# Unsplit f32 scores in every first-layer batch, fewer q/k buffers, more for probabilities, and two rows joined

## The chip, the cores and the metric

One Trainium2 chip, one core of it. The metric is the device time of one execution in microseconds (us); the median of three runs of the kernel before is 391.38 us (390.82 to 391.43).

## What is computed

Two layers of attention on 4 batches of 768 positions. The first has 8 heads of 64: each position sees the 128 positions up to itself and the first 4 ("sinks"). Its output, laid out as 768 x 512, is the input x of the second: 4 experts, each with its own q, k and v of 64, full causal attention, and a gate that keeps the best two experts per position.

```python
# first layer, per head
scores = scale * q @ k.T;  scores = where(is_sink | in_window, scores, -1e9)
a = softmax(scores);       x = a @ v
# second layer, per expert e
q, k, v = x @ wq[e], x @ wk[e], x @ wv[e]
a = softmax(where(causal, -1e9, scale * q @ k.T))
out += (gate weight of e, 0 unless in the top 2) * (a @ v @ wo[e])
```

## The kernel before

**Units.** The 768 positions are 6 row blocks of 128. Heads go in pairs: the two heads (or experts) of a pair sit on partitions 0 to 63 and 64 to 127, and their matmuls use the two halves of TensorE's rows. A first-layer *unit* is one pair of one batch (`first`, L1158; 16 of them), a second-layer unit one pair of experts of one batch (`second`, L1196; 8 of them). `ORD` and `LAST` (L1310) interleave them; in the last batch it is "0 p0 1 2 3 p1 c0 c1", where p is a second-layer unit of batch 2 and c one of batch 3, so the two last units of the program are c0 and c1.

**q and k.** For batches 0 and 1 (`EXACT`, L1306) the first layer uses q and k as they are, as f32: a `Pair` (L709) with `exact` keeps q in its load buffer `qn` and puts k, transposed, in `kx` (batch 0 transposes on TensorE, `turn_by_pe` L774; batch 1 on VectorE, L796). For batches 2 and 3 they are split into a rounded part (type float32r) and the rest: VectorE transposes in place (L800), ACT writes the rounded part (L801), POOL the rest (L805), into `qs` and `ks`. In `scores` (L810) an exact row is one f32 matmul per head (L817), which shows as two instructions in the trace; a split row is three matmuls per head (L822: high by high, high by low, low by high). The second layer always uses split q and k, which `put` (L746) makes from the projections (L1207).

**Rows of the first layer.** Row 0 sees one block, row 1 two (`edge_row`, L1070); rows 2 to 5 go two by two (`both_rows`, L1094). A score row covers 128 columns for row 0 and 260 for the others. Then VectorE adds the mask and takes the row's extreme, ACT takes the exponential, POOL multiplies by the reciprocal of the sum, TensorE transposes the probabilities (L875), ACT or VectorE copies them to `pt` (L704, L706), and TensorE multiplies by the values (L848) into an `acc` bank. One step does this for each row 0 and row 1 in `transposed` (L881).

**Rows of the second layer** (`wide_rows`, L970). Row i sees i+1 blocks. Rows of 5 and 6 blocks have their scores in two parts (`SPLIT`). Where a unit stands in `AWAY` (L1307; the first five second-layer units), rows 4 and 5 (of 5 and 6 blocks) are not transposed on TensorE: `by_way_of_dram` (L942) normalises on POOL into a second `p` buffer, transposes 32 x 32 pieces on VectorE (L958), stores to DRAM (`there`, L959) and loads four parts back (L955), and multiplies straight from `p`. In those units the row group 4 to 5 is done ahead of the group 0 to 3.

**What sets the order.** Nothing is issued in the order of the program text. `Plan` (L346) collects steps with an estimated cost per engine, dependencies, buffers to take and a priority; `emit` (L375) then simulates the engines and takes for each engine the step that can start first, for TensorE the one with the lowest priority after a price for waiting (`HURRY`) and for changing the mode of the array (`STAY`, `BULK`; "rows" for scores, "ROWS" for transposes, "cols" for the products with the values, "FULL"). Each step's priority is moved by a table of hand-set corrections, `NUDGE`. Where TensorE would wait, `emit` puts in multiplications by zero (`fill`, L513). A buffer kind is a ring of so many tiles (`kinds`, L507); a step that needs a new tile waits until all users of the old one are done. DMAs all go through SP's queue.

```python
def score_cost(n, exact=False):
    if exact:
        return 17 + 4 * n / 2.4
    return {128: 284, 256: 355, 260: 359, 384: 524, 512: 697}.get(n, 60 + 1.25 * n)
```

Of the kernel before, what the change touches and what calls it, by code (L numbers as in the profile page):

```python
# [10 lines left out]
F32 = mybir.dt.float32  # L11
F32R = mybir.dt.float32r
# [25 lines left out]
    "busy_PE": -35.2, " ": -14.5, " busy_PE": 44.4, " busy_PE 0": 14.4, "sink_values_DVE": -63.9, " sink_values_DVE": -42.7,  # L38
    "load_SP": -98.1, " load_SP": 27.8, "again_SP": -32.8, " again_SP": 2.5, "sink_values_ACT": -92.2,
    " sink_values_ACT": 34.2, "sink_values_POOL": -20.4, " sink_values_POOL": 18.3, "sink_values_SP": -68.0,  # L40
    " sink_values_SP": -27.3, "weight_ACT": 41.3, " weight_ACT": -64.4, "weight_POOL": -75.8, " weight_POOL": -39.4,
    "000 ": -57.8, "000 load_SP": 33.9, "tr_PE": -4.1, "000 tr_PE": -49.4, "000 tr_PE 0": -108.1, "fn_DVEACT": 23.4,
    "000 fn_DVEACT": 18.5, "000 tr_PE 1": -6.2, "go_POOL": -57.8, "000 go_POOL": 133.7, "000 tr_PE 2": 7.5,
    "000 tr_PE 3": 20.4, "spread_POOL": -50.7, "000 spread_POOL": -8.4, "differences_POOL": 173.3,
    "000 differences_POOL": -37.7, "band_scores_PE": 1.1, "000 band_scores_PE": -64.2, "000 band_scores_PE 0": -75.3,
    "low_DVE": -52.3, "000 low_DVE": 30.9, "exp_ACT": 274.5, "000 exp_ACT": 57.1, "go_DVE": -15.0, "000 go_DVE": 58.1,
    "norm_POOL": -83.7, "000 norm_POOL": 4.7, "000 tr_PE 4": -9.3, "av_PE": 1.6, "000 av_PE": -20.4, "000 av_PE 0": -24.7,
    "000 band_scores_PE 1": 14.2, "000 tr_PE 5": 30.2, "000 av_PE 1": -25.8, "000 band_scores_PE 2": 16.4,
    "pick_DVE": -15.0, "000 pick_DVE": 56.0, "000 band_scores_PE 3": 21.0, "keep_POOL": -105.0, "000 keep_POOL": 9.3,
    "000 tr_PE 6": -6.3, "tri_DVE": -17.0, "000 tri_DVE": -17.4, "of_sinks_PE": -0.7, "000 of_sinks_PE": -10.2,  # L50
# [26 lines left out]
    "110 load_SP": -51.3, "turn_DVE": 119.5, "110 turn_DVE": -77.7, "110 go_POOL": 93.6, "110 spread_POOL": 30.9,  # L77
# [210 lines left out]
}  # L288

HURRY = 29.29  # L290
STAY = 30.56
BULK = -8.87
FILL_COST, FILL_KEEP, FILL_END = 220.0, 0.0, 130000.0
# [177 lines left out]
def kernel(  # L471
# [15 lines left out]
    B, H, S, D = q.shape  # L487
    E = moe_wq.shape[0]
    Dm = H * D
    NB = S // 128  # L490
# [897 lines left out]
```

## Time and profile before

| | |
|---|---|
| median of the runs shown | 391.38 us |
| the profiled execution's own time | 391.6 us |
| its span, first to last instruction | 389.9 us |
| TensorE busy | 381.2 us (98%) |
| VectorE busy | 318.2 us (82%) |
| ACT busy | 263.4 us (68%) |
| POOL busy | 261.5 us (67%) |
| share of the chain that ended last on TensorE | 86% |
| DMA, share of 16 engines | 46.3% |

PE is TensorE's matmuls and PEld its weight loads; DVE is VectorE, ACT ScalarE, POOL GpSimd, SP the engine that issues DMAs. Busy time counts overlapping instructions of one engine once. Matmuls are pipelined: one starts while the one ahead still runs, and their ends are modelled. The chain that ended last follows the work back from the last instruction, at each step to what released it or to the instruction ahead of it on its engine.

### The profile page before, as it was taken

What the parts mean: (1) busy time and instruction counts of PE and PEld (TensorE: products, weight loads), DVE (VectorE), ACT (ScalarE), POOL (GpSimd) and SP (SyncE); (2) the same over time, 40 slices, a digit from 0 to 9 for tenths busy, and PEclk for the clock granted to TensorE, in tenths of its full rate; (3) what the DMA queues carried; (4) which work ended last, traced back from release to release, by engine and by line L of the source; (5) the groups of instructions that cost most, each with busy time, mean ns of one, the idle gap of its engine ahead of it and who ended that gap; (6) DMA issues with size and microseconds to landing.
All of it is one profiled execution on the core that took longest, in us unless ns stands there. A gap on an engine that the chain in (4) does not pass through costs nothing.

```text
span 389.9 us, 12672 instructions
## 1 busy us (share of the span) xinstructions
PE 381.2 (98%) x4276; PEld 318.4 (82%) x4276; DVE 318.2 (82%) x1422; ACT 263.4 (68%) x953; POOL 261.5 (67%) x461
## 2 busy tenths in 40 slices
PE   8999999999999999999998999999999999999996
PEld 7767788978788888878887789978888898987884
DVE  6898996799999889799689977789589826667953
ACT  4898876376988698188589848459778814507740
POOL 4879996378849968658949846499946730039940
PEclk9999999999999999999999999999999999999999
DMA  7979999045865855548915560269000000012003
GB/s 163 227 147 166 192 170 169 0 83 173 193 99 117 234 114 83 81 154 247 200 27 101 133 207 25 42 238 234 32 3 3 3 0 2 3 67 96 3 16 148
DMA packets 138432, 42.84 MB, mean 110 GB/s; under 512 B 122176, under 2 KB 132416, under 8 KB 138368
## 3 DMA queue, kind: packets, MB, share of 16 engines
q1 hardware_dynamic: 138368, 42.04, 46.3%
q8 instruction: 34, 0.56, 0.6%
q14 instruction: 30, 0.25, 0.2%
HBM read 28.25 MB, written 13.50 MB: 107 GB/s over the span
## 4 chain that ended last, share of the span: by engine, by line
PE 86%; ACT 7%; DVE 4%; issue 1%; POOL 0%; DVEq 0%; ACTq 0%
PE acc L848 20%; PE b L1207 18%; PE b L822 12%; PE b L875 9%; PE b L1234 9%; PE b L1281 9%; PE b L817 5%; ACT p L1014 2%; PE acc L852 2%; DVE p L1006 2%; ACT pt L704 1%; ACT p L1115 1%; PE b L1292 1%; PE b L521 1%; DVE p L1111 1%
## 5 line engine op out<-in xcount | busy, mean ns | idle before, releaser
L822 PE MATMUL b<-ks,qs 64*128 64x260 f32 (+4 forms) x672 | 72.6, 325 | 1.1 <-ACT pt L704 0.5
L1014 ACT ACTIVATE p<-p,st 128x128 f32<-128x128 f32 (+5 forms) x96 | 63.6, 668 | 13.6 <-DVE st L1006 13.1
L704 ACT ACTIVATE pt<-b 128x256 f32<-128x256 f32 (+3 forms) x156 | 55.1, 380 | 13.0 <-PE b L875 12.5
L1026 POOL TENSOR_TENSOR p<-p,st 128x128 f32<-128x128 f32 (+5 forms) x76 | 60.8, 823 | 1.3
L822 PEld LDWEIGHTS b<-ks,qs 64*128 64x128 f32 x672 | 52.9, 186 | 7.8 <-ACT pt L704 1.3
L1115 ACT ACTIVATE p<-p,st 128x132 f32<-128x132 f32 x128 | 50.8, 403 | 4.7 <-DVE st L1111 4.3
L875 PE MATMUL b<-ident,p 64*128 64x64 f32 x900 | 47.7, 228 | 0.0
L1006 DVE CUSTOM_DVE_ANT_0 p<-b,cmask 128x384 f32<-128x384 f32 (+3 forms) x96 | 45.3, 504 | 1.3 <-PE b L822 0.9
L875 PEld LDWEIGHTS b<-ident,p 64*128 64x128 f32 x900 | 37.6, 138 | 10.4 <-issue 4.8
L1089 POOL TENSOR_TENSOR p<-p,st 128x256 f32<-128x256 f32 (+1 forms) x32 | 26.4, 834 | 26.8 <-DVE st L864 7.9
L848 PE MATMUL acc<-pt,vn 128*64 128x128 f32 x448 | 42.8, 285 | 0.1
L1234 PE MATMUL b<-wvh,x 128*128 128x260 f32 x192 | 35.9, 285 | 0.0
L1207 PE MATMUL b<-x,wqh 128*128 128x512 f32 (+1 forms) x128 | 33.3, 345 | 0.0
L1111 DVE CUSTOM_DVE_ANT_0 p<-b,pair_mask 128x132 f32<-128x132 f32 x128 | 33.0, 286 | 0.3 <-POOL p L950 0.2
L1281 PE MATMUL b<-woh,y 128*128 128x512 f32 x96 | 32.8, 405 | 0.3 <-DVE st L1006 0.3
L1134 POOL TENSOR_TENSOR p<-p,st 128x512 f32<-128x512 f32 x32 | 33.0, 1041 | 0.0
L1207 PE MATMUL b<-x,wkh 128*128 128x512 f32 (+1 forms) x128 | 32.7, 342 | 0.0
L848 PE MATMUL acc<-pt,v 128*64 128x128 f32 x452 | 31.9, 279 | 0.1
L1082 ACT ACTIVATE p<-p,st 128x128 f32<-128x128 f32 (+1 forms) x64 | 28.7, 452 | 4.6 <-DVE st L1077 4.3
L1108 DVE COPY_PREDICATED b<-earlier,b 128x128 f32<-128x128 int32 x128 | 31.6, 286 | 0.1
L848 PEld LDWEIGHTS acc<-pt,vn 128*64 128x64 f32 x448 | 24.7, 136 | 7.8 <-issue 2.0
L1234 PEld LDWEIGHTS b<-wvh,x 128*128 128x128 f32 x192 | 30.0, 188 | 1.0 <-DVE st L1077 0.3
(136 smaller groups left out, 984.5 us busy)
## 6 DMA issues: line engine op xcount, KB each, us to landing
vn<-in_v_dram SPq DMA_DIRECT2D x32, 192.0 KB, 3.2
out_dram<-o SPq DMA_DIRECT2D x24, 256.0 KB, 2.2
qn<-in_q_dram SPq DMA_DIRECT2D x52, 96.0 KB, 2.4
kn<-in_k_dram SPq DMA_DIRECT2D x52, 96.0 KB, 2.7
there<-p SPq DMA_DIRECT2D x10, 384.0 KB, 3.2
p<-there SPq DMA_DIRECT2D x40, 96.0 KB, 2.4
there<-p SPq DMA_DIRECT2D x10, 320.0 KB, 2.3
p<-there SPq DMA_DIRECT2D x40, 80.0 KB, 2.8
```

What stands on the lines that cost most here:

```text
L704: nc.scalar.activation(dst(), src(), AF.Copy)
L822: nc.tensor.matmul(o, self.qs.t[hs, a, qs], self.ks.t[hs, b, ks], start=n == 0, stop=n == 2)
L848: nc.tensor.matmul(o[e * 64:e * 64 + 64], lhs, rhs, start=e not in self.begun, stop=last and self.done == len(self.steps))
L875: nc.tensor.transpose(t[g].t[:, n, :], x[gs], ident[gs, gs])
L1006: nc.vector.tensor_tensor_reduce(out=one(e)[:, cs], in0=s2[e].t[:, :(c1 - c0) * 128], in1=mask(c0, c1), scale=times, scalar=st.t[:, 3, es] ...
L1014: nc.scalar.activation(x, x, AF.Exp, bias=st.t[:, 0, es], scale=-1.0, accum_out=st.t[:, 1, es])
L1026: nc.gpsimd.tensor_mul(x, x, st.t[:, 2, e:e + 1].to_broadcast([128, n * 128]))
L1111: nc.vector.tensor_tensor_reduce(out=p.t[:, n, :], in0=s2[e].t[:, :SW], in1=pair_mask, scale=-scale, scalar=BIG, op0=OP.add, op1=OP.min, a ...
L1115: nc.scalar.activation(p.t[:, n, :], p.t[:, n, :], AF.Exp, bias=st.t[:, 0, n:n + 1], scale=-1.0, accum_out=st.t[:, 1, n:n + 1])
L1207: nc.tensor.matmul(t.t, w[a][:, c, es], X[b, c].t[:, x, cs], start=c == 0 and m == 0, stop=c == NCH - 1 and m == 2)
L1234: nc.tensor.matmul(t.t[:, :VW], X[b, c].t[:, a, qs], W["wv"][w][:, c, :], start=c == 0 and n == 0, stop=c == NCH - 1 and n == 2)
L1281: nc.tensor.matmul(t.t, Y[b, c].t[:, a, qs], W["wo"][w][:, c, :], start=c == 0 and n == 0, stop=c == EP - 1 and n == 2)
```

## The change

- `EXACT` takes in batches 2 and 3, so all first-layer scores are unsplit f32 matmuls; no first-layer unit uses `qs` or `ks` any more, and each of those two rings shrinks from 2 tiles to 1.
- The ring `p` of probabilities grows from 9 tiles to 13.
- In the five units of `AWAY`, row 3 (of 4 blocks) also goes through DRAM, beside rows 4 and 5.
- In `transposed`, the product step of row 0 is not issued by itself: it is kept in `acc.first` and issued with the step of row 1, in both layers.
- `HURRY`, `STAY` and `BULK` change, and so do nearly all entries of `NUDGE`; the kinds of entries for the splitting steps (`turn_ACT`, `low_POOL`) are gone, those for the joined step (`all_of_PE`) are new.

```diff
...
-HURRY = 29.29
-STAY = 30.56
-BULK = -8.87
+HURRY = 30.54
+STAY = 42.78
+BULK = -14.30
...
-    kinds = {"qn": (3, 768, F32), "kn": (2, 768, F32), "vn": (3, 768, F32), "qs": (2, 2 * S, F32R), "ks": (2, 2 * NB * SW, F32R),
-             "x": (6, 2 * S, F32R), "kx": (2, NB * SW, F32), "v2": (1, 1536, F32), "y0": (1, 2 * S, F32R), "y1": (1, 2 * S, F32R), "p": (9, 768, F32),
+    kinds = {"qn": (3, 768, F32), "kn": (2, 768, F32), "vn": (3, 768, F32), "qs": (1, 2 * S, F32R), "ks": (1, 2 * NB * SW, F32R),
+             "x": (6, 2 * S, F32R), "kx": (2, NB * SW, F32), "v2": (1, 1536, F32), "y0": (1, 2 * S, F32R), "y1": (1, 2 * S, F32R), "p": (13, 768, F32),
...
-            self.begun, self.steps, self.done = set(), [], 0
+            self.begun, self.steps, self.done, self.first = set(), [], 0, None
...
-        def av():
-            acc.done += 1
+        def av(n=n, cols=cols):
             for c, j in enumerate(cols):
                 for e in range(2):
                     acc.add(i, e, value[0](j, e), pt.t[:, 2 * c + e, :], 2 * c + 2 == n)
+        if i == 0 and TOGETHER:
+            acc.first = (av, moved, pt, n, cols)
+            return
+        made, before, pts, many, mine = [av], moved, [pt], n, cols
+        if acc.first:
+            made, before, pts, many, mine = [acc.first[0], av], acc.first[1] + moved, [acc.first[2], pt], n + acc.first[3], [*acc.first[4], *cols]
+            acc.first = None
+
+        def all_of():
+            acc.done += 1
+            for x in made:
+                x()
         new, used = acc.bufs()
-        acc.steps.append(plan.step(prio + AV_LAG, {PE: 109 * n}, av, moved + value[1](cols), new,
-                                   [pt] + value[2] + used, fifo="av", mode="cols"))
+        acc.steps.append(plan.step(prio + AV_LAG, {PE: 109 * many}, all_of, before + value[1](mine), new,
+                                   pts + value[2] + used, fifo="av", mode="cols"))
...
-    EXACT = (0, 1)
-    AWAY, MOVE = {u: (4, 5) for u in ((0, 0), (0, 1), (1, 0), (1, 1), (2, 0))}, 300
+    EXACT = (0, 1, 2, 3)
+    AWAY, MOVE = {u: (3, 4, 5) for u in ((0, 0), (0, 1), (1, 0), (1, 1), (2, 0))}, 300
+    TOGETHER = True
```

## Rows read from the trace of the kernel before

**Rows 1.** The page: the span; busy us, share of the span, instructions.
```profile
span 389.9 us, 12672 instructions
...
PE 381.2 (98%) x4276; PEld 318.4 (82%) x4276; DVE 318.2 (82%) x1422; ACT 263.4 (68%) x953; POOL 261.5 (67%) x461
```

**Rows 2.** Busy time by stretch, the last 22 us; the first line names the columns.
```profile
core 0: us, PE busy (x) PEld busy (x) DVE busy (x) ACT busy (x) POOL busy (x), PEclk, DMA share, GB/s
368.00:390.00 22.00, 18.16 (x206) 14.22 (x204) 11.32 (x27) 5.91 (x15) 6.08 (x7) 0.98 0.20 73
```

**Rows 3.** Timeline of TensorE: start, length, instruction; long score rows alone, L817 and L822.
```profile
64.65 0.71 PE L817 MATMUL b<-kx,qn 64*128 64x260 f32 x4
65.19 0.22 PE L875 MATMUL b<-ident,psk 64*128 64x64 f32 x2
...
138.08 0.63 PE L822 MATMUL b<-ks,qs 64*128 64x260 f32 x6
138.55 0.46 PE L875 MATMUL b<-ident,p 64*128 64x64 f32 x10
```

**Rows 4.** Groups of TensorE by form: count | busy us, mean ns | idle before.
```profile
L817 PE MATMUL b<-kx,qn 64*128 64x260 f32 x160 | 26.1, 408 | 0.1
...
L822 PE MATMUL b<-ks,qs 64*128 64x260 f32 x240 | 23.3, 305 | 0.2 <-DVE st L1077 0.2
```

**Rows 5.** Timeline of TensorE, short score rows alone.
```profile
63.61 0.49 PE L817 MATMUL b<-kx,qn 64*128 64x128 f32 x4
63.94 0.41 PE L875 MATMUL b<-ident,p 64*128 64x64 f32 x8
...
136.96 0.55 PE L822 MATMUL b<-ks,qs 64*128 64x128 f32 x6
137.35 0.37 PE L875 MATMUL b<-ident,p 64*128 64x64 f32 x6
```

**Rows 6.** Groups by form, POOL and ACT: the splitting of q.
```profile
L805 POOL TENSOR_TENSOR qs<-qn,qs 128x384 fp32r<-128x384 f32 x16 | 16.2, 1014 | 4.0 <-ACT qs L801 4.0
...
L801 ACT ACTIVATE qs<-qn 128x384 fp32r<-128x384 f32 x16 | 8.2, 516 | 0.0
```

**Rows 7.** Timeline of TensorE, 330 to 333 us: transposes and products in runs.
```profile
330.01 0.96 PE L875 MATMUL b<-ident,p 64*128 64x64 f32 x24
330.78 0.77 PE L822 MATMUL b<-ks,qs 64*128 64x384 f32 x6
331.49 1.53 PE L848 MATMUL acc<-pt,v 128*64 128x128 f32 x24
332.95 0.46 PE L875 MATMUL b<-ident,p 64*128 64x64 f32 x8
333.22 0.59 PE L822 MATMUL b<-ks,qs 64*128 64x384 f32 x4
```

**Rows 8.** Groups by form, VectorE: transposes on the way through DRAM.
```profile
L958 DVE STREAM_TRANSPOSE p<-p 128x640 f32<-128x640 f32 x10 | 8.3, 828 | 0.0
```

**Rows 9.** Busy time by stretch, 78 to 127 us, columns as in rows 2.
```profile
78.00:127.00 49.00, 48.79 (x589) 39.34 (x586) 48.22 (x216) 39.53 (x149) 37.77 (x67) 1.00 0.59 133
```

**Rows 10.** The DRAM tile: its issues on SP, ns min/median/max; time to landing.
```profile
L955 SPq DMA_DIRECT2D p<-there x80: 303/430/1963, 91.1 to 271.3; - x80
L959 SPq DMA_DIRECT2D there<-p x20: 319/344/1153, 88.0 to 262.7; - x20
...
DMA to landing us min/median/max: 2.0/2.6/5.2
```

**Rows 11.** Timeline of TensorE, 351.6 to 353.2 us: a lone step of row 0.
```profile
351.69 0.60 PE L822 MATMUL b<-ks,qs 64*128 64x256 f32 x6
352.36 0.44 PE L848 MATMUL acc<-pt,v 128*64 128x128 f32 x4
352.73 0.62 PE L822 MATMUL b<-ks,qs 64*128 64x256 f32 x6
353.19 0.28 PE L875 MATMUL b<-ident,p 64*128 64x64 f32 x4
```

**Rows 12.** Busy time by stretch of line L1207 alone; PE, PEld, clock, DMA.
```profile
308.00:325.00 17.00, 17.00 (x96) 14.60 (x96) 1.00 0.00 1
```

More of the change, by code (lines that the diff above doesn't have):

```diff
@@ L37 @@
 NUDGE = {
[L38 to L47, printed above, removed]
@@ L48 @@
-    "000 band_scores_PE 1": 14.2, "000 tr_PE 5": 30.2, "000 av_PE 1": -25.8, "000 band_scores_PE 2": 16.4,
-    "pick_DVE": -15.0, "000 pick_DVE": 56.0, "000 band_scores_PE 3": 21.0, "keep_POOL": -105.0, "000 keep_POOL": 9.3,
-    "000 tr_PE 6": -6.3, "tri_DVE": -17.0, "000 tri_DVE": -17.4, "of_sinks_PE": -0.7, "000 of_sinks_PE": -10.2,
[26 rows of a table removed]
-    "110 load_SP": -51.3, "turn_DVE": 119.5, "110 turn_DVE": -77.7, "110 go_POOL": 93.6, "110 spread_POOL": 30.9,
[20 rows of a table removed]
-    "most_DVE": -123.6, "001 most_DVE": -1.2, "rank_POOL": 48.2, "001 rank_POOL": 26.8, "values_ACT": -124.6,
@@ L99 @@
-    "001 values_ACT": -18.0, "weigh_DVE": -107.5, "001 weigh_DVE": -60.0, "proj_PE": -8.3, "001 proj_PE": -16.4,
[5 rows of a table removed]
-    "001 factor_POOL": 87.0, "001 norm_POOL": -120.4, "by_way_of_dram_DVE": -34.9, "001 by_way_of_dram_DVE": -73.8,
-    "by_way_of_dram_SP": -39.1, "001 by_way_of_dram_SP": 69.0, "back_SP": -58.9, "001 back_SP": -1.1, "001 av_PE": 13.4,
[30 rows of a table removed]
-    "turn_ACT": -12.9, "210 turn_ACT": 14.9, "low_POOL": 90.7, "210 low_POOL": 8.9, "210 go_POOL": -18.8,
[150 rows of a table removed]
-}
-HURRY = 29.29
-STAY = 30.56
-BULK = -8.87
+    "busy_PE": 33.5, " ": -40.9, " busy_PE": -16.2, " busy_PE 0": -17.8, "sink_values_DVE": -16.4,
@@ new lines @@
+    " sink_values_DVE": -55.9, "load_SP": 13.5, " load_SP": 92.9, "again_SP": 2.2, " again_SP": -33.1,
+    "sink_values_ACT": 70.0, " sink_values_ACT": -18.8, "sink_values_POOL": -19.7, " sink_values_POOL": -20.8,
+    "sink_values_SP": -9.5, " sink_values_SP": 1.4, "weight_ACT": 56.9, " weight_ACT": 25.6, "weight_POOL": 64.1,
+    " weight_POOL": -72.7, "000 ": -24.6, "000 load_SP": -68.6, "tr_PE": -1.3, "000 tr_PE": -25.9, "000 tr_PE 0": -51.6,
+    "fn_DVEACT": 41.8, "000 fn_DVEACT": -67.8, "000 tr_PE 1": -26.1, "go_POOL": -128.5, "000 go_POOL": -52.9,
@@ new lines @@
+    "000 tr_PE 2": 11.5, "000 tr_PE 3": 12.1, "spread_POOL": 72.3, "000 spread_POOL": 21.3, "differences_POOL": 139.4,
+    "000 differences_POOL": -18.7, "band_scores_PE": 1.9, "000 band_scores_PE": -43.2, "000 band_scores_PE 0": -2.3,
+    "low_DVE": 3.9, "000 low_DVE": -146.7, "exp_ACT": 300.6, "000 exp_ACT": -4.8, "go_DVE": 6.8, "000 go_DVE": -34.9,
[3 rows of a table added]
+    "tri_DVE": -18.1, "000 tri_DVE": 108.8, "of_sinks_PE": 0.4, "000 of_sinks_PE": -4.3, "000 of_sinks_PE 0": 6.5,
[47 rows of a table added]
+    "most_DVE": 89.8, "001 most_DVE": 48.2, "rank_POOL": 224.3, "001 rank_POOL": -59.8, "values_ACT": -79.4,
@@ L293 @@
+    "001 values_ACT": 24.7, "weigh_DVE": -61.0, "001 weigh_DVE": 68.2, "proj_PE": 7.3, "001 proj_PE": -6.9,
[5 rows of a table added]
+    "001 factor_POOL": 15.7, "001 norm_POOL": -46.2, "by_way_of_dram_DVE": -6.4, "001 by_way_of_dram_DVE": 3.5,
+    "by_way_of_dram_SP": -85.0, "001 by_way_of_dram_SP": 12.0, "back_SP": -83.2, "001 back_SP": -164.3, "001 av_PE": -3.8,
[175 rows of a table added]
+}
+HURRY = 30.54
+STAY = 42.78
+BULK = -14.30
 FILL_COST, FILL_KEEP, FILL_END = 220.0, 0.0, 130000.0
```

461 rows, old and new, of the table NUDGE are left out of this document.

## The prediction

> **What bounds the kernel now.** I read the page's busy times first: TensorE is busy 381.2 of 389.9 us [rows 1]. Then the table by stretch, where the last 22 us hold 18.2 of work and the granted clock stands at 0.98 to 1.00 of 2.4 GHz [rows 2, 9, 12]: 3.7 of the 8.7 idle us are the tail, and 5.0 us are left for the start and all waits between. The time is what TensorE has to do, plus a start and a tail, and an edit is worth what it takes from TensorE or adds to it. Time freed on ACT or POOL is worth something only inside those 5.0 us.
>
> TensorE time is read in the timeline as the distance from one start to the next: ends of matmuls overlap, starts don't.
>
> **Unsplit scores in batches 2 and 3.** Eight pairs of heads have one short row (128 columns) and five long ones (260) each. A long row alone, a transpose behind it, takes 65.19-64.65 = 0.54 us unsplit and 138.55-138.08 = 0.47 split: +0.07 [rows 3]. That is the one like-for-like pair, so I take it: 40 x 0.07 = +2.8. From above: unsplit matmuls last 408 ns in the mean, split ones 305 [rows 4]; if all of that 0.10 counted once per row, +4.1. From below: with four matmuls in place of six, nothing. A short row takes 63.94-63.61 = 0.33 unsplit, 137.35-136.96 = 0.39 split [rows 5]: 8 x -0.06 = -0.5. Together +2.3, bounds -0.5 and +4.1.
>
> The Trainium skill ("FP8 and Floating Point Precision", TensorE Precision Notes) says that a true FP32 matmul makes four passes through the array. Against the three products of the split this rule speaks against the edit: a third more than 0.47 is an estimate of +0.16 per long row, and with a third on short rows too some +7 us in place of +2.3. The lone rows of both lengths disagree with it in size; a mild form of it is a rival below.
>
> The splitting itself goes: 32 copies of 0.51 us on ACT and 32 subtractions of 1.01 us on POOL (those of qs stand in [rows 6], those of ks are as many and as long), 16 and 32 us. VectorE's transposes of q and k stay. TensorE waited little for any of it: bounds 0 and the 5.0 us of start and waits; I take -0.5, as most of the 5.0 must be the start, before anything is split. That q now stays in its load buffer until its scores are done delays later loads of q, which are issued a whole unit ahead: nothing, and a load's 2 to 5 us if that lead is gone.
>
> **Rows of 4 blocks through DRAM.** In five units such a row loses 16 transposes. 24 take 330.78-330.01 = 0.77, 8 take 333.22-332.95 = 0.27 [rows 7], so 16 take 0.50: 5 x 0.50 = -2.5. The bound beyond is -3.2, if a change of mode goes with each (0.13, below). The products behind them stay, in number and shape. New beside TensorE, per row: two VectorE transposes, two stores and eight loads on SP's queue; the two POOL multiplications write elsewhere but are as many. A transpose of 640 columns takes 0.83 [rows 8], so one of 512 some 0.66: +6.6 for ten on VectorE, against ten copies of 512 columns that go, from VectorE or ACT. VectorE has no room from 78 to 127, where two of these units lie (48.2 busy of 49 [rows 9]), and ACT has 9.5 us there: bounds 0 and +6.6, I take +0.5, because copies can move to ACT. SP issues a store in 0.34 and a load in 0.43 us [rows 10]: 2 x 0.34 + 8 x 0.43 = 4.1 per row. Behind them on that queue stand loads of q, k and v for the next units, issued a unit ahead, so nothing; without that lead 4.1 per unit. Row 3 is the last row of these units, and its part of y can't be finished until it is back from DRAM; the first-layer units that follow cover that.
>
> **Rows 0 and 1 in one step.** 17 of the 24 steps of row 0 (4 matmuls) stand alone between other modes, like the one at 352.36. It takes 352.73-352.36 = 0.37 [rows 11]. 24 in a run take 332.95-331.49 = 1.46 [rows 7], 0.061 each, so four more in a run cost 0.24: 0.13 is saved. The score ahead of it also pays: 352.36-351.69 = 0.67 into products, 353.19-352.73 = 0.46 into a transpose, so up to 0.21 more [rows 11]. 17 x 0.13 = 2.2 and 17 x 0.34 = 5.8 are the bounds; I take 0.20 each, -3.4, nearer the lower one, since not every lone step has a score ahead. The joined step waits for the copies of row 1 and holds two of three pt buffers until then; what is late next is a third transpose, and scores cover it.
>
> **One qs, one ks, 13 p.** Only the 8 second-layer units still use qs and ks. In batch 3 two of them follow each other; both are now projected in one stretch, 17 us from 308 on, 8.5 each [rows 12]. With one buffer the last projection must come behind the last score of the unit ahead, which now starts at 352.73 [rows 11]. A unit's scores take 2 x 1 + 4 x 2 = 10 buffers of p; nine were one too few, and 13 let these scores run on at 335. So the wait is covered by work that can change places (values and stores stand between). Bounds 0 and +8.5; I take 0.
>
> **The order** (new priorities, a change of mode priced at 42.8 for 30.6) is in no row. With some 90 stretches of products in the trace, one in ten more or fewer is 9 x 0.34 = 3.1 us either way. I take -0.5.
>
> Sum: +2.3 - 0.5 - 2.5 + 0.5 - 3.4 + 0 - 0.5 = -4.1. The profiled execution took 391.6, so 387.5; the median of the runs is 0.2 lower, so I forecast 387.3 us.
>
> **Rivals.** *Slower: the single buffers bind at the end.* Place: batch 3, from 325 on. If the scores of the unit ahead still end at 353, the last unit's projection starts there, its scores come 8.5 us later than now, and the tail behind them has nothing to run beside. It decides once other TensorE work that is ready there falls short. For it: the last 22 us already lack work [rows 2]. Against it: ten p are fewer than 13. 387.3 + 8.5 = 395.8, and slower once more than 4.9 of it is paid. Chance 0.14.
>
> *VectorE becomes the bound from 78 to 127* [rows 9]. There the transposes of two rows are paid (4 x 0.66 = 2.6) and their TensorE gain of 1.0 is lost; with the 0.5 already in the sum, +3.1: 390.4. With some four joined steps of that stretch (0.8) lost too, 391.2. Chance 0.10, taken as no change.
>
> *Dear scores.* Long rows at +0.10 and no gain in short ones: +4.1 for +2.3, 389.1. The Trainium skill's rule on FP32 passes, cited above, would give more, some 392 as an estimate. Chance 0.13, still faster.
>
> *More relief.* Freed POOL and ACT and four more p end all waits (-5.0 for -0.5) and the order is one in ten better: 387.3 - 4.5 - 2.6 = 380.2; half of it, 383.8. Chance 0.13. Against it: there is little waiting to end.
>
> That the change does not do what it says can be in one place: if the order put rows 0 and 1 together at little cost anyway, the 3.4 are not there, 390.7; that belongs to "no change".
>
> **How the numbers follow.** The forecast has 0.50. This kernel's measurement tells about 0.2% (0.8 us) from no change. Faster 0.50 + 0.13 + 0.13 = 0.76; within 0.10; slower 0.14. The range reaches from 383.0, inside the relief rival, to 392.3, past the VectorE rival into the slower one; left out are some 0.06 below and 0.12 above.
>
> **What would show it.** Right: no ACT or POOL line splits q or k; the unsplit group grows from 160 to 320 matmuls of 260 columns and the split one is gone; 80 fewer transposes of p; lone steps of four products nearly gone; TensorE's busy time about 4 us lower, with its idle time unchanged. Wrong: TensorE idle or on filler after 335 ahead of a projection; VectorE at its limit with TensorE waiting for it; a lone unsplit long row far from 0.54; as many changes of mode as now.

## The result and the profile after

The kernel after takes 387.44 us in the median of 4 runs (387.10 to 387.83), beside 391.33 for the kernel before. The ratio is 0.9902, with a 95% interval of 0.9888 to 0.9917: faster by 1.0%. The forecast was 387.3 us.

The page of the kernel after, the lines that answer to [rows 1]:

```profile
span 385.4 us, 12301 instructions
...
PE 375.7 (97%) x4124; PEld 315.0 (82%) x4124; DVE 317.5 (82%) x1416; ACT 252.7 (66%) x927; POOL 230.0 (60%) x429
```

TensorE is busy 5.5 us less; its idle time went from 8.7 to 9.7 us. VectorE has as much to do as before. ACT lost 10.7 us and POOL 31.5.

The groups by form that answer to [rows 4] and [rows 8], TensorE, then POOL and VectorE (count | busy us, mean ns | idle before):

```profile
L811 PE MATMUL b<-kx,qn 64*128 64x260 f32 x320 | 51.8, 410 | 0.6 <-POOL kx L763 0.3 <-ACT kx L698 0.3
L869 PE MATMUL b<-ident,p 64*128 64x64 f32 x820 | 43.0, 228 | 0.0
L842 PE MATMUL acc<-p,v 128*64 128x128 f32 x300 | 19.6, 276 | 0.9 <-DMA p<-there 0.9
...
L955 POOL TENSOR_TENSOR p<-p,st 128x512 f32<-128x512 f32 x10 | 10.2, 1040 | 0.7 <-PE b L869 0.6
...
L963 DVE STREAM_TRANSPOSE p<-p 128x512 f32<-128x512 f32 x10 | 7.0, 704 | 1.7 <-POOL p L955 1.4
```

All 320 long score matmuls are unsplit, and no split group of 260 columns is left. Two of TensorE's lone score rows, a long and a short one, with the transposes behind them, answer to [rows 3, 5]:

```profile
99.25 0.71 PE L811 MATMUL b<-kx,qn 64*128 64x260 f32 x4
99.79 0.28 PE L869 MATMUL b<-ident,p 64*128 64x64 f32 x4
...
191.31 0.44 PE L811 MATMUL b<-kx,qn 64*128 64x128 f32 x4
191.58 0.28 PE L869 MATMUL b<-ident,p 64*128 64x64 f32 x4
```

From start to start these are 0.54 and 0.27 us. The stretches that answer to [rows 9, 2], and between them the one in which the single qs and ks were to bind:

```profile
core 0: us, PE busy (x) PEld busy (x) DVE busy (x) ACT busy (x) POOL busy (x), PEclk, DMA share, GB/s
78.00:127.00 49.00, 47.97 (x590) 39.51 (x588) 47.12 (x206) 38.17 (x143) 35.84 (x64) 1.00 0.59 151
320.00:342.00 22.00, 22.00 (x176) 19.90 (x175) 12.30 (x49) 7.57 (x21) 1.29 (x5) 1.00 0.10 37
363.50:385.50 22.00, 18.15 (x223) 14.78 (x218) 9.01 (x20) 6.21 (x16) 5.71 (x6) 1.00 0.19 73
```

TensorE is full from 320 to 342, VectorE has 1.9 us of room in its densest stretch, and the tail is as it was. TensorE's waits after the change:

```profile
PE b L1297 <- DVE lanes L560: 1.1, 1, 1.1
PE acc L846 <- DVE x L686: 0.9, 1, 0.9
PE acc L842 <- DMA p<-there: 0.9, 1, 0.9
PE acc L842 <- DVE pt L700: 0.7, 1, 0.7
PE b L869 <- DMA kn<-in_k_dram: 0.5, 1, 0.5
```

No wait is for qs, ks or the splitting of q and k. This is where TensorE's time went: the distances from one matmul's start to the next, added up by kind over the whole trace (a wait counts with the matmul ahead of it):

| kind of matmul | before, us | after, us | difference |
| --- | --- | --- | --- |
| scores of 128 and 260 columns, split and not | 51.8 (x528) | 53.3 (x432) | +1.5 |
| other split scores | 37.9 | 37.1 | -0.8 |
| transposes | 45.5 (x1060) | 42.8 (x980) | -2.8 |
| products | 88.8 | 87.1 | -1.7 |
| sinks | 9.2 | 8.3 | -1.0 |
| projections, values, stores | 140.8 | 139.8 | -1.0 |
| fillers | 6.0 (x76) | 8.0 (x100) | +1.9 |
| matmuls on zeros at the start | 4.6 | 3.8 | -0.8 |

Before rounding they add up to -4.5 us. The first line holds 80 long rows, 42.5 us before and 43.3 after, and 24 short ones, 9.3 and 10.1. The last line is no work of the change: in another trace of the kernel after, with three psk buffers (below), the same 20 matmuls take 4.6 us again. Stretches of one mode went from 348 to 298, stretches of products from 89 to 71, and the 17 lone steps of four products are gone.

### The profile page after: what moved, and what is told of

Its sections match the earlier page's. It is cut to its first block, busy times and chain, and to the rows that moved or that the text cites. A ratio compares the mean times of both kernels' runs of the same rounds, so it can differ in the third digit from the quotient of the medians.

```text
span 385.4 us, 12301 instructions
## 1 busy us (share of the span) xinstructions
PE 375.7 (97%) x4124; PEld 315.0 (82%) x4124; DVE 317.5 (82%) x1416; ACT 252.7 (66%) x927; POOL 230.0 (60%) x429
## 4 chain that ended last, share of the span: by engine, by line
PE 76%; DVE 15%; ACT 3%; DMA 2%; issue 2%; SPq 1%; POOL 0%; DVEq 0%; ACTq 0%; POOLq 0%
PE b L1212 18%; PE acc L842 14%; PE b L1239 9%; PE b L1286 9%; PE b L811 9%; PE b L869 7%; PE b L816 6%; DVE p L1011 3%; DVE b L1113 2%; DVE p L1116 2%; DVE pt L924 1%; DVE x L686 1%; DVE p L963 1%; PE acc L846 1%; DMA kn<-in_k_dram 1%
## 5 line engine op out<-in xcount | busy, mean ns | idle before, releaser
L1019 ACT ACTIVATE p<-p,st 128x640 f32<-128x640 f32 (+5 forms) x96 | 63.7, 667 | 10.0 <-DVE st L1011 8.8
L811 PE MATMUL b<-kx,qn 64*128 64x260 f32 (+1 forms) x384 | 58.1, 393 | 0.8 <-ACT kx L698 0.4
L698 ACT ACTIVATE pt<-b 128x256 f32<-128x256 f32 (+2 forms) x158 | 53.3, 368 | 7.9 <-PE b L869 7.8
L1031 POOL TENSOR_TENSOR p<-p,st 128x128 f32<-128x128 f32 (+5 forms) x66 | 50.4, 787 | 0.6
L816 PE MATMUL b<-ks,qs 64*128 64x384 f32 (+3 forms) x384 | 45.2, 344 | 0.3 <-DVE st L1011 0.2
L869 PE MATMUL b<-ident,p 64*128 64x64 f32 x820 | 43.0, 228 | 0.0
L811 PEld LDWEIGHTS b<-kx,qn 64*128 64x128 f32 x384 | 34.8, 186 | 8.4 <-issue 1.2
L955 POOL TENSOR_TENSOR p<-p,st 128x640 f32<-128x640 f32 (+2 forms) x30 | 36.9, 1254 | 1.3 <-PE b L869 0.6
L816 PEld LDWEIGHTS b<-ks,qs 64*128 64x128 f32 x384 | 32.4, 186 | 4.8 <-issue 1.2
L1212 PE MATMUL b<-x,wkh 128*128 128x256 f32 (+1 forms) x128 | 33.4, 347 | 0.2 <-DVE st L1116 0.2
```

Source lines behind the costliest of these rows:

```text
L698: nc.scalar.activation(dst(), src(), AF.Copy)
L811: nc.tensor.matmul(o, self.q_of()[hs, qs], self.ks.t[hs, 0, ks], start=True, stop=True)
L816: nc.tensor.matmul(o, self.qs.t[hs, a, qs], self.ks.t[hs, b, ks], start=n == 0, stop=n == 2)
L869: nc.tensor.transpose(t[g].t[:, n, :], x[gs], ident[gs, gs])
L1019: nc.scalar.activation(x, x, AF.Exp, bias=st.t[:, 0, es], scale=-1.0, accum_out=st.t[:, 1, es])
L1031: nc.gpsimd.tensor_mul(x, x, st.t[:, 2, e:e + 1].to_broadcast([128, n * 128]))
```

## The experiments

In all but the first two, the order of the steps on each engine is the one recorded from the kernel named, and only the steps of the edit differ, placed where their inputs are ready or at a place given to them; so an edit meets the order of a kernel that was laid out without it. The first two keep the kernel's own planner, whose estimates don't count the second issue. "+x us" is against the kernel of that order: before as measured beside it, after as 0.9902 times that.

**What a score row costs.** The scores of the 40 long rows of batches 2 and 3 are issued twice, in each kernel:

```diff
-        lambda: pair.scores(...)
+        def scores_of():
+            for _ in range(2 if pair.twice and i else 1):
+                pair.scores(...)
```

> The kernel before, with the split scores of the 40 long first-layer rows of batches 2 and 3 issued twice in a row (same order otherwise, same output). Theory (TensorE's own work sets the time): each row adds its price in a run, six matmuls at some 0.35 us, so 40 x 0.35 = +14 us, about 405. Rival (TensorE has hidden room, other engines set the time): under half of that, below 398.

> The changed kernel, with the unsplit scores of the same 40 rows issued twice. Theory: the unsplit row is dearer than the split one by 0.07 to 0.10 us, so this adds 40 x 0.42 to 0.45 = 17 to 18 us, about 405, which is 2.8 to 4 more than the split rows add to the kernel before. If the four passes of f32 set the price, 4/3 of what the split rows add, 4.7 more. If the unsplit row is no dearer in a run, the same addition as in the kernel before.

Measured: 403.17 us split twice (ratio to before 1.0299, 1.0284 to 1.0313), +11.65 us or 0.29 a row; 400.80 us unsplit twice (1.0239, 1.0223 to 1.0256), +13.1 us or 0.33 a row. Both are less than was expected (14, and 17 to 18). In the two groups by form the count is right:

```profile
L822 PE MATMUL b<-ks,qs 64*128 64x260 f32 x480 | 36.1, 289 | 0.0
```

```profile
L811 PE MATMUL b<-kx,qn 64*128 64x260 f32 x480 | 67.7, 397 | 0.6 <-POOL kx L763 0.3 <-ACT kx L698 0.3
```

TensorE sets the time in both kernels: of the 12.5 and 15.8 us that its trace grew by from start to start, 11.65 and 13.1 came into the time. A row behind its like is dearer unsplit by 0.04 us of time (13.1/40 - 11.65/40), and by 0.08 from start to start (15.8/40 in the one trace, 12.5/40 in the other). For 40 rows that is 1.5 to 3.2 us, with the forecast's +2.8 for long rows inside. In the kernel after itself, where most rows don't stand behind their like, the long rows together rose by 0.7 us.

**What a transpose costs.** In the kernel after, the transposes of the three rows of 4 blocks that still go through TensorE are issued four times:

```diff
-            for m in range(n):
+            for m in [*range(n)] * (4 if n == 8 else 1):
                 turned(t, m, block(m % 2, m // 2))
```

> The kernel after, in its own order, with the 16 transposes of each row of 4 blocks that still goes through TensorE (three units) issued four times over into the same PSUM: 3 x 48 = 144 more. Theory (a transpose costs what the runs of them show, 0.77 us for 24, and TensorE sets the time): +4.6 us, 392.1. Rival (the 10.4 us that came with the 80 transposes of the five rows put back, 0.13 each, is the price of the transposes themselves): +18.7 us, 406. Rival (transposes hide beside other work): 387.5.

Measured: 391.88 us (1.0015, 1.0006 to 1.0024), +4.4 us for 144, or 0.030 each. The 80 transposes that the change removes are worth 2.4 us. (The rival's 10.4 us belong to the run with one part undone, further down; counted as here they are 10.8.)

**What a lone step costs.** In the kernel after, the steps of row 0 are issued by themselves again, at places given to them; 14 of the 24 then stand alone:

```diff
-    TOGETHER = True
+    TOGETHER = False
```

> The changed kernel in its own order, but in 14 of the 24 units the four products of row 0 are issued by themselves ahead of row 1's, between work of other modes. Theory: a stretch of products by itself costs 0.13 to 0.34 us, 0.20 as forecast, so 14 x 0.20 = +2.8 us, about 390.2 (389.2 to 392.2). Rival (the joining itself is worth little, the new order brought the gain): under +0.7, below 388.1.

Measured: 390.44 us (0.9975, 0.9964 to 0.9986), +2.8 us, 0.20 a step. Stretches of products went from 71 to 85 and TensorE's waits fell, from 5.9 to 4.4 us, so no new wait is in the price. TensorE's busy time grew by 4.6 us in this trace, more than came into the time; so 0.20 is what a lone step costs the kernel, and not all that it costs TensorE. One of these steps, with the score ahead of it:

```profile
201.98 0.88 PE L1078 MATMUL b<-ks,qs 64*128 64x384 f32 x6
202.79 0.44 PE L1104 MATMUL acc<-pt,vn 128*64 128x128 f32 x4
203.16 0.62 PE L1078 MATMUL b<-ks,qs 64*128 64x384 f32 x4
```

**What the splitting costs.** In the kernel after, ACT and POOL get the splitting of q and k back, first into one scratch tile:

```diff
+    scratch = consts.tile([128, 384], F32R, name="scratch")
 ...
+                if self.loaded:
+                    h = plan.step(prio, {ACT: ...}, lambda: nc.scalar.activation(w3, part(0), AF.Copy), steps, (), [x])
+                    plan.step(prio, {POOL: ...}, low, [h], (), [x])
 ...
+        pair.loaded = b >= 2
```

> The changed kernel in its own order, with the work of the removed splitting given back to ACT and POOL: for every transposed q and k of batches 2 and 3 a copy of 384 columns on ACT and a subtraction on POOL into a scratch tile that nothing reads. Theory: freed time on ACT and POOL is worth 0.5 us, so about 387.9 (387.4 to 388.4). Rival (the relief carries the gain): +3 us and more, 390.5 or above.

Measured: 405.95 us (1.0366, 1.0350 to 1.0382), far above what was expected. Part of it was the edit's own: over the shared tile ACT waited 13.5 us for POOL and POOL 15.1 us for ACT, whose copy the subtraction reads. So each engine got a tile of its own, with one buffer of psk (small tiles with the probabilities of the sinks) less for room, and that buffer was tried alone. In this version the subtraction doesn't read ACT's copy and takes 0.83 us for 1.01:

> The kernel after, in its own order, with the splitting work of before put back on ACT and POOL for the first-layer units of batches 2 and 3 (a copy and a subtraction of 384 columns for every transposed q and k), this time into a scratch tile for each engine, so that neither waits for the other; to make room psk has three buffers in place of four. Theory (the relief of ACT and POOL is worth nothing that can be measured, and the 405.95 us of the kernel with one shared scratch tile came from the waits over that tile): 387.5 to 388.5 us, TensorE's waits within 1 us of the 5.9 of the kernel after. Rival (the order stands only because ACT and POOL were relieved): 392 us or more, with TensorE waiting for ks and qs as it did with the shared tile.

> The kernel after, in its own order, with three buffers of psk in place of four and nothing else: it tells whether the 7.9 us of the kernel with the splitting put back beside two scratch tiles (395.4 us), which also had three, came from the splitting. Theory (from the splitting: psk is a tile of 128 columns that is read once and early): 387.5 us, within 0.8. Rival (the fourth psk carries the order): 391 us or more, TensorE waiting for psk or POOL for its buffers.

Measured: 395.40 us with the splitting (1.0110, 1.0096 to 1.0123) and 387.46 us with three psk alone (0.9893, 0.9876 to 0.9909). The psk costs nothing; the splitting costs 7.9 us in this order. The 392 us of the rival are passed; what TensorE waits for is another matter. The timeline of all engines around TensorE's longest wait shows the way it takes:

```profile
136.23 0.83 POOL L1062 TENSOR_TENSOR scratch<-kx 128x384 f32<-128x384 f32 x1
...
137.14 0.83 POOL L1062 TENSOR_TENSOR scratch<-qn 128x384 f32<-128x384 f32 x1
...
137.92 1.04 POOL L1226 TENSOR_TENSOR p<-p,st 128x512 f32<-128x512 f32 x1
...
138.99 0.71 DVE L1234 STREAM_TRANSPOSE p<-p 128x512 f32<-128x512 f32 x1 [1.97 <-POOL p L1226]
139.63 0.98 DVE L1015 TENSOR_TENSOR ks<-b,ks 128x512 fp32r<-128x512 f32 x2
...
140.34 0.48 PE L1082 MATMUL b<-kx,qn 64*128 64x260 f32 x1 [2.40 <-DVE ks L1015]
```

Two subtractions stand on POOL ahead of the multiplication of a 4-block row; VectorE's transpose of that row waits 1.97 us for it; the subtraction for ks, queued behind that transpose, reads its PSUM bank late; and TensorE, which needs the bank, waits 2.40 us. A second wait of TensorE, 1.35 us at 233, has the same chain ahead of it. VectorE's waits for POOL's multiplications on the way through DRAM go from 1.7 us with three psk alone to 7.5, and TensorE's waits grow by 4.2; the rest of the 7.9 us was not traced further. So in this order it is the freed POOL that lets a third row per unit go by DRAM without holding VectorE up. That a kernel whose order was laid out with the splitting in it would lose as much is not shown; no such kernel was run.

**One part alone, in the order of before.** Unsplit scores in all batches:

```diff
-    EXACT = (0, 1)
+    EXACT = (0, 1, 2, 3)
```

> The kernel before, in its own order, with unsplit scores in batches 2 and 3 alone (two buffers of qs and ks, nine of p, rows 0 and 1 apart; a step moves only where its kx buffer isn't free yet). Theory: the unsplit scores cost TensorE 2.3 us and freeing ACT and POOL gives 0.5 back, so +1.8 us, about 393.3 (391 to 395). Rival (the freed 48 us on ACT and POOL carry the gain of the change): faster than the kernel before by 1 us or more.

Measured: 419.60 us (1.0731, 1.0709 to 1.0754), +28.5 us, against every expectation. VectorE's wait, the load it waits for, and TensorE's wait, from the waits of VectorE and the timelines of SP's queue, VectorE and TensorE:

```profile
DVE qn L1064 <- DMA qn<-in_q_dram: 17.6, 5, 4.6
...
190.59 2.02 SPq L1443 DMA_DIRECT2D qn<-in_q_dram  x4
...
194.51 1.04 DVE L1064 STREAM_TRANSPOSE qn<-qn 128x384 f32<-128x384 f32 x2 [4.27 <-DMA qn<-in_q_dram]
...
196.00 0.80 PE L1475 MATMUL b<-x,wkh 128*128 128x512 f32 x1 [4.54 <-DVE st L1379]
```

TensorE's last unsplit scores of the unit start at 189.42; the next load of q is issued at 190.59, when they have read its buffer. VectorE stands before the transpose of that q until 194.51, and what TensorE needs from VectorE stands behind it. Three pauses like it, each with VectorE at a load of q for 4.3 to 4.6 us, are 14.4 of the 16.2 us by which TensorE's waits grew. Much of the rest is the clock, by stretch of TensorE (busy, granted clock, then the DMA columns):

```profile
188.00:192.00 4.00, 3.46 (x35) 1.00 0.58 176
192.00:196.00 4.00, 0.00 (x0) 0.70 1.11 206
196.00:200.00 4.00, 4.00 (x12) 0.50 0.84 172
200.00:204.00 4.00, 4.00 (x21) 0.94 0.00 0
```

The granted clock fell to 0.50, the lower of its two levels (1.2 GHz), while TensorE stood still and came back some 4 us after work resumed. The mean of this run is 0.974, against 0.999 before, but part of the low clock falls in the pauses, where it costs nothing. TensorE's busy time in stretches of half a microsecond, times the share of the clock that is missing in each, adds up to 7.0 us of full speed. Of the 27.2 us by which the span grew some 4 are left; they were not traced.

Rows of 4 blocks through DRAM alone:

```diff
-    AWAY, MOVE = {u: (4, 5) for u in (...)}, 300
+    AWAY, MOVE = {u: (3, 4, 5) for u in (...)}, 300
```

> The kernel before, in its own order as far as buffers allow, with the rows of 4 blocks of the five units through DRAM; their products stand at the next run of products that the transfers can reach. Theory: -2.5 us of transposes and +0.5 on VectorE, so -2 us, about 389.5 (388.5 to 391). Rival (with nine p the second buffers of these rows hold up other steps): slower than the kernel before.

Measured: 421.73 us (1.0780, 1.0761 to 1.0799), +30.6 us. TensorE's waits, SP's queue and TensorE's timeline for one row:

```profile
PE acc L1115 <- DMA p<-there: 14.1, 5, 4.8
...
112.52 0.76 SPq L1226 DMA_DIRECT2D there<-p  x1
115.16 1.73 SPq L1222 DMA_DIRECT2D p<-there  x4
...
118.68 1.12 PE L1115 MATMUL acc<-p,v 128*64 128x128 f32 x8 [4.79 <-DMA p<-there]
```

From the issue of the store to the products is 6.2 us, and the order of before has the products where the transposed row used to be ready. Five products wait like this, 14.1 of the 19 us by which TensorE's waits grew, and the clock falls here too (0.976 in the mean; 7.9 us of full speed by the same sum). The rival's direction came true; whether nine p had a part in it was not tried.

Rows 0 and 1 joined alone, in the seven units whose steps can be put together in that order:

```diff
+        if i == 0 and plan.part in TOGETHER:
+            acc.first = (av, moved, pt, n, cols)
+            return
...
+    TOGETHER = ('001', '020', '030', '101', '110', '120', '210')
```

> The kernel before, in its own order, with rows 0 and 1 joined in seven units (of the 16 whose row-0 step stood alone), where the three pt buffers allow it without another order. Theory: 7 x 0.20 = -1.4 us, about 390.1 (389.1 to 390.6). Rival (joined steps wait for row 1 and give it back): no change or slower.

Measured: 393.53 us (1.0056, 1.0043 to 1.0069), +2.4 us where -1.4 was due by the price of 0.20. TensorE's waits add up to 7.2 us for 4.9, in small pieces:

```profile
PE acc L1150 <- ACT sk L1002: 1.0, 2, 0.8
PE b L1115 <- ACT pt L1002: 0.7, 1, 0.7
PE b L1120 <- ACT pt L1002: 0.5, 1, 0.5
```

**One part undone, in the order of after.** The five rows of 4 blocks go through TensorE again:

```diff
-    AWAY, MOVE = {u: (3, 4, 5) for u in (...)}, 300
+    AWAY, MOVE = {u: (4, 5) for u in (...)}, 300
```

> The changed kernel, in its own order as far as buffers allow, with the rows of 4 blocks of the five units transposed on TensorE again, each beside another run of transposes. Theory: five times 16 transposes, 0.50 us each, come back and VectorE gets its 0.5 back: +2 us, about 389.5 (388.5 to 390.6). Rival (the way through DRAM gave nothing, because VectorE or the transfers took its place): 387.7 or less.

Measured: 398.08 us (1.0178, 1.0162 to 1.0195), +10.8 us. The 80 transposes are 2.4 of it by their measured price, and TensorE's waits grew by 4.7; what the other 3.7 are was not settled. It isn't the price of transposes in a run, which is the 0.030 above.

**A version that might beat both.** The one TensorE wait of the kernel after that a change of two steps could fill was tried: the products at 117.2 go behind the scores that follow them.

```
after:  transposes, products of the DRAM row, transposes, sinks, scores, products
here:   transposes, transposes, sinks, scores, products of the DRAM row, products
```

> The kernel after, in its own order but for one step: the 8 products of a row from DRAM, for which TensorE waits 0.87 us at 117.2, are issued behind the next transposes, sinks and scores, straight ahead of the next products; nothing else moves. Theory (TensorE's order sets the time, and a wait that is filled comes back in full): 0.87 us of wait and one stretch of products (0.20) less, 386.4 us. Rival (the step is late for all that comes behind it, and the wait turns up elsewhere): 387.5 us, or some tenths more.

Measured: 388.83 us (0.9937, 0.9925 to 0.9950), 1.3 us slower than after. The timeline of TensorE there, and its clock by stretch:

```profile
115.85 0.63 PE L1131 MATMUL b<-ident,p 64*128 64x64 f32 x9
117.06 0.33 PE L1131 MATMUL b<-ident,p 64*128 64x64 f32 x3 [0.58 <-DVE st L1273]
117.64 0.43 PE L1108 MATMUL acc<-sk,vs 64*128 64x128 f32 x2 [0.25 <-ACT sk L960]
...
114.00:117.00 3.00, 2.48 (x35) 1.00 0.37 97
117.00:120.00 3.00, 2.69 (x27) 0.73 0.78 125
120.00:123.00 3.00, 3.00 (x38) 0.70 0.00 0
```

The next transposes weren't ready either: 0.58 + 0.25 = 0.83 us of waits stand for the 0.87. And the clock was 0.73 and 0.70 for 6 us, which is 1.7 us of full speed, where the same stretches of the kernel after had 1.00. That can't be all that makes this version slower: in three of its five executions the mean clock was 0.999 or 1.00, and they took 388.13 to 388.83 us, all above the 387.5 of the kernel after. What they lose was not found. The wait for the DRAM row itself isn't in every execution: it shows with 1.0 us in the trace with three psk and not at all in that with four times the transposes. No version that beats the kernel after came out of these runs.

## Why the prediction was right, and where its steps were not

**The bound.** It holds. 40 long rows more on TensorE cost 0.29 or 0.33 us each, 144 transposes 0.030 each.

**Scores, +2.3.** The table gives +1.5, by terms that came out otherwise: the long rows +0.7 for +2.8, the short ones +0.8 (0.4 of it a wait) for -0.5. The lone long row into a transpose measured 0.54 against 0.47, as taken; over all its places the unsplit long row takes 0.54 in the mean after, the split one 0.51 before. The lone short row took 0.33 and 0.27 us unsplit and 0.39 split; over all places a short row takes 0.39 before and 0.42 after, so the lone pair did not stand for the rest. The lower bound of -0.5 was not reached. The four-pass rule of the Trainium skill ("FP8 and Floating Point Precision", TensorE Precision Notes) would have a third more than the split. In a run of like rows the trace shows 0.394 for 0.313 us, which is 1.26 times, close to it. In the mix of this kernel it is 53.3 for 51.8 us. So the rival of dear scores fell; why the long rows lose less in the mix than in a run is not shown.

**Relief, -0.5.** The gain is not seen: TensorE's waits went from 4.9 to 5.9 us. The step that doesn't hold in the order of after is the sentence that time freed on ACT or POOL is worth something only inside the 5.0 us of start and waits: with the splitting put back that order is 7.9 us slower, and in the waits that were followed POOL then comes late to the row of 4 blocks. There relief and that row belong together, and the two were priced one by one. But other edits too cost more than their price in an order made without them (joined rows +2.4 where -1.4 was due), so the 7.9 us need not be what the relief is worth to a kernel laid out with the splitting in it. That stays open.

**Rows of 4 blocks, -2.5 and +0.5.** TensorE's part is right: 0.030 x 80 = 2.4, and -2.8 in the table. VectorE's ten transposes took 0.70 each for the estimated 0.66, 7.0 us in all; its copies to `pt` fell by 5.0, and its busy time as a whole by 0.7. That the trip through DRAM is covered holds in the order of after, with one wait of 0.9 us; in the order of before it cost 14.1 us. "Nothing" was right for this order and not for the edit.

**Joined rows, -3.4.** Right: 0.20 a step was measured on 14 of them. Products, sinks and the split scores of the second layer fell by 1.7, 1.0 and 0.8 us in the table; 0.5 of the 0.8 are waits.

**The load buffers of q, nothing.** The text put 2 to 5 us on it if the loads' lead is gone. In the order of before it is gone, and VectorE's five waits for q are 17.6 us, 3.5 each. In the kernel after, no wait of TensorE is for q, and one of 0.5 us for k.

**Single qs and ks, 0.** Right: TensorE is busy 22.00 of 22.00 us from 320 to 342, no wait is for qs or ks, and the last multiplication by zero is at 86 us. The rival in which they bind at the end fell, and with it the one of VectorE, which has 47.12 of 49 us to do from 78 to 127, less than before.

**The order, -0.5 within 3.1.** 50 fewer stretches of one mode; 18 of them are stretches of products. In the table the projections and the zeros at the start are 1.8 us shorter (the zeros in this trace alone), and the fillers 1.9 longer, neither of which was forecast; they cancel.

So the bound, the transposes and the joined rows were right, two terms were mis-sized (scores 0.8 too high, and what the order brings) and one was priced without the row that it belongs to (relief). That the forecast came within 0.2 us is partly luck: the long and the short rows, the waits, the fillers and the projections were each off by 1 us or more, and the errors cancel. Either of two parts alone in the order of before costs 28 to 31 us, though their TensorE prices are +2.3 and -2.5. No part was tried in an order laid out for it, and the 13 p, the single qs and ks and the new priorities were not tried alone; how the 3.9 us divide among them is shown only as far as the prices above go.

## What to carry to other kernels

Where one engine is full, price an edit by what that engine issues, and test the price by issuing the work again: here a transpose (0.030 us) and a lone step (0.20) came out as forecast, and a score row at 0.29 and 0.33 for the 0.35 and 0.42 expected. One lone pair of rows is not the price of a form in all its places. The sum of such prices was near the gain in the kernel whose order was laid out anew for all the edits; put alone into an order that was made without it, an edit that looked small made the full engine wait, and the lower clock after each pause added to the bill. Before calling time freed on a side engine worthless, look at what another edit adds to that engine's queue, and who stands behind it.

## What the runs showed of the hardware that was not expected

With one part alone in the order of before, the granted clock fell to 0.50 in pauses of TensorE of 3.3 to 5.0 us and came back 4 to 6 us after work resumed; it took 7.0 us of full speed with unsplit scores alone and 7.9 with the rows of 4 blocks. Idle time of nearly the same length (0.87 us in one piece, 0.83 in two) left the clock at 1.00 in the kernel after and came with 0.70 to 0.73 for 6 us in the kernel with the later product, whose mean clock was 0.996 in two executions and 0.999 or 1.00 in three. Why the one and not the other was not tried. The step from one scratch tile to two was worth 10.5 us (405.95 to 395.40), though not by the tile alone: with one, ACT and POOL waited for each other's use of it for 28.6 us together; with two, the subtraction had no data of ACT's to wait for and was 0.18 us shorter.
